# Windowed attention with a gated projection: each value product issued in three steps, one warm-up fewer, and a new written-out order

## The chip, the cores and the metric

The kernel runs on one core of one Trainium2 chip. The metric is the device time of one execution in microseconds (us). Five engines work side by side, each strictly in its own order: PE (matrix products; its weight loads are listed apart as PEld), DVE (vector), ACT (activations), POOL (here only a few fills at the start) and SP (issues the loads and most stores).

## What is computed

```
# attention: 8 batches, 8 heads, 512 local and 32 global positions, head size 64
s_g   = q_g @ [k_g, k_l].T / 8 ;      out_g = softmax(s_g) @ [v_g, v_l]
s_ll  = q_l @ k_l.T / 8, only where |i - j| <= 32
out_l = softmax([q_l @ k_g.T / 8, s_ll]) @ [v_g, v_l]
x     = [out_g, out_l] with the heads side by side        # 8 x 544 x 512
# gated projection
gate  = sigmoid(sum over k of conv_w[k] * x shifted by k)  # causal, 5 taps
out   = (gate * (x @ w_val)) @ w_out                       # 512 x 512 each
```

All of it is float32, but for `w_val`, `w_out` and `conv_w`, which arrive as float64 and are put into float32 parts by the kernel itself.

## The kernel before, in words

**Units of work.** The 64 pairs of batch and head are handled as 32 units `u` (two heads each, 128 partitions) and 16 windows `w` of two units. For a unit, PE makes the local scores (`s`, L385, and 8 mask products at L391 that stand at its end), DVE takes the maxima (`mx`, L396), ACT the exponentials (`exp`, L406), ACT or DVE scales them (`norm`, L421 or L423), and DVE transposes them in blocks of 32 (`t`, L429). For a window PE then makes the value product (`av`, L440): 160 small matrix instructions, each with a weight load of its own, one after the other over the ten slots of values. Copies take the result to SBUF (`xc`), it is split into a high and a low part (`xh`, `xl`, L489), and the five-tap convolution runs on DVE (`tap`, `conv`, L494). For units 0 and 1 alone PE makes the convolution (`pc`, L510) with diagonals that ACT writes (`dg`).

**Global queries.** Per batch: scores `gs` (L314), maximum `gmax` (L321, L322), exponentials `gexp` (L325), transposes on PE `gt` (L331) and their copies `gtc`, product with the values `gav` (L347), division `gden`, `grec`, `gnorm`, one more transpose `gx`.

**Weight products.** `g1.b.e.t` (L531) and `g2.b.r.e` (L555) are the two projections: three passes of 128x512 (high by high, low by high, high by low) per task, 280 tasks in all, most of the time of PE. Between them stand `gv`, `gh`, `gl` on DVE and ACT, and behind them the copies `ob` and the stores `st`. Before the first one can run, the two weight matrices are put together from their float64 words, eight tiles `w0` to `w7`, each by five steps on DVE (`s0` to `s4`, L206 to L214; `s0` may go to ACT, L204), a copy `high` and a difference `low` (L283).

**Order.** Nothing schedules itself. One long string of task names, `ORDER` (L60 to L148), is walked from front to back (L681), and each engine gets its instructions in that order. An `@` behind a name gives the PSUM banks of the task (of eight), and `:ACT` or `:DVE` the engine where a task may run on either. A load is issued on SP, and waits for the last PE instruction that stands ahead of it in the string (L245). `av` holds four half-used PSUM banks from its first instruction until both `xc` copies have read them. The names beginning with `z` are products of zeros (L624): they compute nothing, and are there to occupy PE. Two stand in the string of before, of six instructions each; two more stand ahead of it (L679).

```
        for name, *_ in LINE:
            if name[0] == "z":
                zeros(int(name.partition(".")[0][1:]), HOME[name][0])
            else:
                tasks[name]()
```

Of the kernel before, what the change touches and what calls it, by code (L numbers as in the profile page):

```python
# [61 lines left out]
gs0@06 w0.s1 rec1 w0.s2 gmax0 norm1.1:DVE ig2 iq4 exp0.0 exp3.0 exp0.1 w0.s3 iq5 norm1.0:ACT s2@2 den0 w1.s0:DVE gexp0.0
gt0.0@0 rec0 w0.s4 w0.high:ACT norm0.1:ACT t1 w0.low gtc0.0:ACT gexp0.1 ig3 exp3.1 norm0.0:DVE w1.s1 mx2 t0 gt0.1@0
w1.s2 w2.s0:DVE exp2.0 gtc0.1:ACT den3 w2.s1 rec3 w2.s2 w1.s3 w2.s3 norm3.1:DVE av0@46 exp2.1 den2 ig0 ig1 wi5 w2.s4
norm3.0:ACT xc0:ACT s5@0 w1.s4 xc1:ACT rec2 halo0 pc0.0@6 pc0.1 w2.high:ACT w1.high:ACT mx5 s4@2 w1.low iq7 norm2.1:ACT
w3.s0:ACT exp5.0 norm2.0:DVE t3 pc0.2 w2.low mx4 xh0:ACT w5.s0:DVE gav0@7 exp5.1 pc0.3 iq6 gden0 pc0.4 exp4.0 t2
conv0.3:ACT exp4.1 w3.s1 xl0 den5 grec0 av1@04 rec5 pc1.0@6 w3.s2 w5.s1 norm5.1:ACT w3.s3 xc3:ACT den4 w5.s2 wi6 w3.s4
ig6 wi4 rec4 gnorm0 xc2:ACT w3.high:DVE xh1:DVE s6@2 gs1@04 pc1.1 ig4 pc1.2 iv2 norm5.0:ACT norm4.0:ACT mx6 gmax1 xl1
gx0@7 exp6.0 gexp1.0 w3.low pc1.3 w5.s3 gexp1.1 gxc0:ACT tap2:ACT halo1:ACT pc1.4 exp6.1 ig5 tap3:DVE g1.0.2.0@7
g1.0.0.3@4 gt1.0@0 s7@2 iq9 conv2.0 iv3 w5.s4 w4.s0:ACT conv3.0 iq8 den6 conv1.3:ACT fix0 g1.0.1.2@5 t5 norm4.1:ACT  # L70
g1.0.3.3@6 rec6 gtc1.0:ACT mx7 norm6.0:ACT g1.0.2.2 g1.0.0.0 g1.0.1.0 exp7.0 conv2.1 w4.s1 conv3.1 w4.s2 t4 w5.high:ACT
w5.low g1.0.0.2 gt1.1@0 w4.s3 g1.0.1.3 g1.0.0.1 exp7.1 fix1 g1.0.1.1 gtc1.1:ACT conv3.2 w4.s4 g1.0.3.1 ig7 den7 av2@02
wi7 iq10 sig0 g1.0.2.3 g1.0.3.0 conv2.2 conv3.3 w4.high:ACT conv2.3 rec7 gv.0.1 norm6.1:ACT w6.s0:DVE xc4:ACT gv.0.0
sig1 s8@0 norm7.0:ACT xc5:ACT gh.0.0:ACT gav1@4 t6 ig11 w4.low iq11 mx8 g1.0.3.2 gl.0.0 g1.0.2.1 exp8.0 gden1 w7.s0:DVE
grec1 exp8.1 ig8 w7.s1 s9@2 gv.0.3 gnorm1 norm7.1:ACT mx9 ig9 gv.0.2 gs2@04 tap5:ACT gmax2 g2.0.3.0@6 t7 w6.s1 exp9.0
ig10 w7.s2 w6.s2 iv5 g2.0.0.0@7 den8 gexp2.1 gexp2.0 g2.0.3.1 g2.0.0.1 gx1@4 iq13 gxc1:ACT w7.s3 exp9.1 w6.s3 rec8
av3@04 gh.0.1:ACT den9 norm8.1:ACT w6.s4 tap4:DVE xc7:ACT halo2:ACT norm8.0:DVE rec9 g2.0.2.0@2 w7.s4 w6.high:ACT
g2.0.1.0@3 xc6:ACT g2.0.2.1 gl.0.1 iv4 conv4.0 gt2.0@4 t8 w6.low w7.high:ACT g2.0.1.1 gt2.1@0 iq12 gtc2.0:ACT w7.low
norm9.1:ACT xh2:ACT s10@4 g2.0.1.2 mx10 gtc2.1:ACT conv4.1 g2.0.2.2 g2.0.2.3 conv5.0 norm9.0:ACT halo3:ACT g2.0.3.2
exp10.0 xl2 g2.0.1.3 ob.0.1:ACT ob.0.2:ACT gav2@0 g2.0.0.2 exp10.1 g1.1.1.0@1 t9 conv5.1 conv4.2 g1.1.1.1 gden2 tap7:ACT  # L80
conv5.2 av4@24 den10 conv4.3 conv5.3 xh3:ACT grec2 rec10 sig2 g2.0.0.3 xc8:ACT tap6:DVE st.0.2:SP g2.0.3.3 xl3 st.0.1:SP
ob.0.0:ACT norm10.1:DVE gnorm2 s11@2 g1.1.0.2@0 conv6.0 xc9:ACT ob.0.3:ACT s13@4 g1.1.1.3 g1.1.0.3 mx11 s12@6
norm10.0:ACT st.0.3:SP iq14 st.0.0:SP t10 mx13 exp11.0 exp11.1 conv7.0 mx12 den11 exp13.0 g1.1.1.2 conv6.1 ig13 g1.1.0.0
gx2@2 iq15 g1.1.0.1 gxc2:DVE rec11 conv6.2 exp12.0 g1.1.2.1@3 exp13.1 norm11.1:DVE norm11.0:DVE conv6.3 t11 g1.1.2.0
exp12.1 g1.1.3.3@2 g1.1.3.1 conv7.1 den12 conv7.2 rec12 g1.1.2.2 conv7.3 g1.1.3.0 xh4:ACT sig3 av5@46 ig12 g1.1.2.3
xc11:ACT ig15 gv.1.1 g1.1.3.2 xc10:ACT gv.1.0 den13 norm12.1:ACT gh.1.0:DVE norm12.0:ACT gv.1.2 gs3@06 gl.1.0 iv6 iq16
s15@3 gv.1.3 g2.1.3.0@5 ig14 gmax3 g2.1.1.0@2 g2.1.3.1 gexp3.0 g2.1.1.1 gh.1.1:DVE gexp3.1 gt3.0@0 gt3.1@6 xh5:ACT rec13
gtc3.0:ACT norm13.0:ACT gtc3.1:ACT gl.1.1 g2.1.1.2 halo4:DVE tap8:ACT t12 g2.1.3.2 mx15 xl5 norm13.1:ACT s14@0 g2.1.3.3
conv8.0 g2.1.2.0@6 gav3@7 g2.1.2.1 ob.1.3:ACT tap9:ACT mx14 st.1.3:SP g2.1.0.0@5 t13 gden3 conv9.0 exp15.0 g2.1.1.3
grec3 conv9.1 iv7 iq17 exp14.0 g2.1.0.1 g2.1.2.2 exp15.1 gnorm3 g1.2.1.2@7 exp14.1 xl4 conv8.1 tap10:DVE conv9.2 conv8.2  # L90
g2.1.0.2 g1.2.1.1 gx3@3 gxc3:ACT ob.1.1:ACT den14 g1.2.1.3 halo5:ACT av6@03 conv9.3 tap11:ACT rec14 st.1.1:SP conv8.3
sig4 g2.1.2.3 ob.1.2:ACT g1.2.1.0 xc12:ACT xc13:ACT norm14.1:DVE g1.2.3.2@2 den15 conv11.0 s16@0 rec15 conv10.0
norm15.1:DVE norm15.0:ACT norm14.0:DVE gv.2.1 tap13:ACT mx16 s17@3 mx17 conv10.1 iq18 t15 g1.2.3.3 g1.2.0.0@7 g1.2.2.0@6
exp16.0 conv10.2 exp16.1 t14 conv11.1 exp17.0 ig18 g1.2.2.1 g1.2.3.1 st.1.2:SP iq19 g1.2.3.0 ig19 exp17.1 g1.2.2.3
g1.2.0.3 tap12:ACT conv10.3 g1.2.0.2 conv11.2 ig16 conv11.3 sig5 g2.1.0.3 av7@03 xc15:ACT xc14:ACT xh6:DVE g1.2.2.2
g1.2.0.1 den16 xl6 gv.2.3 gv.2.2 gv.2.0 xh7:ACT g1.3.1.0@4 gs4@02 xl7 gmax4 tap15:ACT halo6:ACT s18@6 ob.1.0:ACT
gh.2.0:ACT iv8 gexp4.1 mx18 iq21 iq20 rec16 st.1.0:SP gexp4.0 den17 ig17 g1.3.0.0@5 g1.3.1.1 gh.2.1:DVE gl.2.0 g1.3.1.2
g1.3.1.3 g1.3.0.1 halo7:ACT gt4.0@0 g1.3.0.3 norm16.1:ACT gtc4.0:ACT gl.2.1 conv13.0 conv12.0 tap14:DVE g2.2.3.0@2
exp18.0 conv12.1 exp18.1 s19@0 g2.2.0.0@3 g2.2.0.1 norm16.0:ACT rec17 mx19 norm17.1:ACT conv13.1 iq23 den18 t16 gt4.1@6
gtc4.1:ACT g2.2.0.2 g2.2.3.1 conv13.2 g2.2.3.2 conv12.2 norm17.0:ACT g2.2.3.3 exp19.0 ob.2.3:ACT t17 gav4@6 g2.2.0.3  # L100
conv13.3 conv15.0 conv12.3 exp19.1 conv15.1 ob.2.0:ACT conv14.0 gden4 g2.2.1.0@7 rec18 sig6 g2.2.1.1 conv14.1 grec4
den19 g1.3.0.2 g2.2.1.2 st.2.3:SP gnorm4 av8@02 ig20 norm18.1:ACT conv15.2 rec19 xc16:ACT iv9 xc17:ACT g1.3.3.1@6
g2.2.1.3 g1.3.3.3 conv14.2 gx4@2 norm19.0:DVE ig22 ob.2.1:ACT s21@0 st.2.1:SP norm19.1:ACT gv.3.1 conv15.3 s20@3 gv.3.0
g2.2.2.0@5 conv14.3 mx20 gxc4:ACT iv11 g1.3.3.2 norm18.0:ACT t19 sig7 exp20.0 g2.2.2.1 iq22 st.2.0:SP g2.2.2.2 g1.3.3.0
exp20.1 t18 gv.3.3 g1.3.2.0@2 mx21 g1.3.2.1 den20 halo8:ACT exp21.0 tap17:DVE g2.2.2.3 exp21.1 gh.3.0:DVE av9@63 gl.3.0
tap16:DVE g1.3.2.2 g1.3.2.3 xc19:ACT gs5@03 xc18:ACT rec20 conv16.0 norm20.1:DVE den21 gv.3.2 gmax5 iv10 xh8:ACT
gh.3.1:ACT s23@6 ob.2.2:ACT g2.3.3.0@2 g2.3.2.0@5 gl.3.1 st.2.2:SP g2.3.2.1 ig21 gexp5.1 iq26 mx23 rec21 gexp5.0 gt5.0@0
g2.3.2.2 ig23 halo9:ACT conv16.1 norm20.0:ACT t20 tap19:DVE norm21.0:DVE g2.3.3.1 xh9:ACT iq25 g2.3.2.3 g2.3.3.2 s22@3
exp23.0 gtc5.0:ACT conv17.0 ob.3.2:ACT mx22 norm21.1:ACT g2.3.3.3 xl9 g2.3.0.0@5 conv17.1 exp23.1 gt5.1@0 gtc5.1:ACT
iq24 g2.3.0.1 g2.3.0.2 ob.3.3:ACT t21 gav5@0 g2.3.0.3 exp22.0 st.3.2:SP conv17.2 st.3.3:SP xl8 conv16.2 iq27 den23  # L110
exp22.1 g1.4.0.2@1 den22 g2.3.1.0@2 g1.4.0.1 av10@36 g2.3.1.1 gden5 rec22 tap18:ACT grec5 rec23 ob.3.0:ACT conv18.0
g1.4.0.0 norm23.1:DVE gnorm5 conv17.3 norm23.0:ACT conv16.3 g2.3.1.2 conv19.0 norm22.1:DVE norm22.0:ACT xc20:ACT s24@3
st.3.0:SP ig27 ig25 conv18.1 xc21:ACT t22 s25@5 mx24 g1.4.0.3 sig8 mx25 g1.4.1.2@7 g1.4.1.1 gv.4.0 t23 exp24.0 conv19.1
conv19.2 g2.3.1.3 conv18.2 g1.4.1.3 conv18.3 exp24.1 ob.3.1:ACT exp25.0 den24 g1.4.1.0 conv19.3 av11@03 exp25.1
tap21:ACT iv13 g1.4.2.3@2 gv.4.1 gx5@5 xc23:ACT rec24 g1.4.2.2 g1.4.3.1@7 xc22:DVE gxc5:DVE tap22:DVE norm24.1:DVE
# [632 lines left out]
```

## Time and profile before

| What | us |
|---|---|
| median of 3 runs | 357.73 (355.07 to 360.5) |
| the profiled execution | 357.83 |
| its span, first to last instruction | 354.9 |
| outside the span | 2.9 |

The busy shares of the engines are taken over the span. PE runs its instructions in a pipeline, so that a PE that counts as busy need not be at its peak. "issue" as the end of a wait stands for time in which an engine waited for nothing that the profile shows.

### The profile page before, as it was taken

To read this page: it belongs to the slowest core of one execution; us is meant where nothing else is said; L and a number is where in the kernel's file an instruction comes from. 1 tells how busy PE (TensorE), PEld (TensorE's weight loads), DVE (VectorE), ACT (ScalarE), POOL (GpSimd) and SP (SyncE) were. 2 spreads that over 40 slices of the span, in tenths; PEclk is the share of its full clock that TensorE was granted. 3 is DMA by queue.
4 is the path that set the end of the run, shared out by engine and by line. 5 is a ranking of instruction groups with operands and counts; after the bars stand their busy time and mean duration, and the time that the engine had idled before them with its cause. 6 is when DMAs were issued, how large, how long until landed. Compare 5 with 4: busy or idle time off the path is not lost.

```text
span 354.9 us, 15327 instructions
## 1 busy us (share of the span) xinstructions
PE 328.3 (93%) x6736; PEld 255.5 (72%) x6736; DVE 304.5 (86%) x545; ACT 278.6 (78%) x887; POOL 1.0 (0%) x8
## 2 busy tenths in 40 slices
...
GB/s 278 376 234 43 178 102 267 243 220 265 159 64 125 195 180 175 100 216 125 225 128 258 149 268 136 86 144 209 170 116 21 175 154 86 2 30 31 60 89 90
DMA packets 19603, 54.75 MB, mean 154 GB/s; under 512 B 2128, under 2 KB 4560, under 8 KB 19536
## 3 DMA queue, kind: packets, MB, share of 16 engines
...
q8 instruction: 52, 0.85, 1.0%
...
## 4 chain that ended last, share of the span: by engine, by line
PE 72%; DVE 15%; ACT 5%; issue 4%; DMA 2%; SPq 0%; ACTq 0%; DVEq 0%
PE psum L555 23%; PE psum L531 22%; PE psum L440 10%; PE psum L385 7%; DVE gate L494 3%; PE psum L347 3%; DMA qk<-in_qk_dram 2%; DVE pts L429 2%; DVE mx L396 2%; PE psum L331 2%; PE psum L314 2%; PE psum L510 2%; DVE gm L321 1%; ACT pm L406 1%; DVE xl L489 1%
## 5 line engine op out<-in xcount | busy, mean ns | idle before, releaser
L406 ACT ACTIVATE pm<-psum,mx 128x128 f32<-128x128 f32 x256 | 90.7, 397 | 4.3 <-DVE mx L398 4.1
L494 DVE SCALAR_TENSOR_TENSOR gate<-xc,cw,gate 128x512 f32<-128x512 f32 x120 | 85.9, 741 | 1.4 <-ACT gate L230 1.1
L406 ACT ACTIVATION_READ_ACCUMULATOR pm<-psum,mx 128x1 f32 x256 | 60.5, 236 | 0.0
L555 PE MATMUL psum<-woh,gh 128*128 128x512 f32 x128 | 53.3, 416 | 0.0
L531 PE MATMUL psum<-xh,wvh 128*128 128x512 f32 x128 | 53.1, 415 | 0.0
L421 ACT ACTIVATE pm<-pm,mx 128x128 f32<-128x128 f32 x164 | 52.4, 413 | 0.4 <-DVE mx L415 0.4
L531 PE MATMUL psum<-xh,wvl 128*128 128x512 f32 x128 | 50.4, 394 | 0.0
L531 PE MATMUL psum<-xl,wvh 128*128 128x512 f32 x128 | 50.3, 393 | 0.0
L396 DVE TENSOR_REDUCE mx<-psum 128x8 f32<-128x1024 f32 x32 | 38.9, 1216 | 13.2 <-PE psum L391 13.2
L555 PE MATMUL psum<-woh,gl 128*128 128x512 f32 x128 | 50.2, 392 | 0.0
L555 PE MATMUL psum<-wol,gh 128*128 128x512 f32 x128 | 50.1, 392 | 0.0
L440 PEld LDWEIGHTS psum<-pts,v 32*64 32x64 f32 x2560 | 38.0, 135 | 15.1 <-issue 8.2
L440 PE MATMUL psum<-pts,v 32*64 32x96 f32 (+3 forms) x2560 | 42.8, 266 | 6.5 <-issue 5.4
L385 PE MATMUL psum<-qk 64*32 64x128 f32 x2048 | 38.1, 278 | 2.5 <-DMA qk<-in_qk_dram 1.3
L429 DVE STREAM_TRANSPOSE pts<-pm 128x1024 f32<-128x1024 f32 x32 | 39.6, 1238 | 0.2 <-ACT pm L421 0.2
L385 PEld LDWEIGHTS psum<-qk 64*32 64x32 f32 x2048 | 31.1, 107 | 11.8 <-issue 6.1
L555 PEld LDWEIGHTS psum<-woh,gh 128*128 128x128 f32 x128 | 24.1, 188 | 7.4 <-issue 2.2
L531 PEld LDWEIGHTS psum<-xh,wvh 128*128 128x128 f32 x128 | 24.0, 188 | 7.4 <-issue 1.6
L538 DVE TENSOR_TENSOR gv<-psum,gate 128x512 f32<-128x512 f32 x32 | 21.8, 685 | 7.8 <-PE psum L531 5.3
L236 ACT COPY ob<-psum 128x512 f32<-128x512 f32 x29 | 17.2, 601 | 14.2 <-PE psum L555 10.9
L531 PEld LDWEIGHTS psum<-xh,wvl 128*128 128x128 f32 x128 | 24.0, 188 | 5.7
L555 PEld LDWEIGHTS psum<-woh,gl 128*128 128x128 f32 x128 | 24.0, 188 | 5.4
(103 smaller groups left out, 485.1 us busy)
## 6 DMA issues: line engine op xcount, KB each, us to landing
...
```

Source lines behind the costliest of these rows:

```text
L236: A.copy(out, in_)
L347: on_pe(T.matmul(global_av(b)[SG * c:SG * c + SG, h, :], pgt[:, h, a, SG * c:SG * c + SG], vt[:, a, h, :], start=(a == 0), stop=(a == GS - ...
L385: on_pe(T.matmul(s[h][C * j:C * j + C, P * i:P * i + P], qkt[rows, C * m:C * m + C], keys, start=(i == 0), stop=False))
L396: V.tensor_reduce(out=mx[:, :8], in_=banks(f"s{u}", 2).rearrange("p h (i c) -> p (h i) c", i=R), axis=AX.X, op=ALU.max, negate=True)
L406: A.activation(out=pm[:, h, i, :], in_=st[u]["s"][h][:, P * i:P * i + P], func=AF.Exp, bias=mx[:, c:c + 1], scale=SCALE, accum_out=mx[:, 8 ...
L421: A.activation(out=p[:, i, :], in_=p[:, i, :], func=AF.Copy, scale=rec[:, i:i + 1])
L429: V.transpose(out=st[w, "pts"][:, :, R * k:R * k + R].rearrange("p h i a q -> p h (i a q)"), in_=st.pop(u)["pm"].rearrange("p h i c -> p h ...
L440: on_pe(T.matmul(x[j // 2][D * h:D * h + D, j % 2, C * first:C * (first + count)], vt[rows, slot, h, :], p, start=(slot == 0), stop=stop))
L494: V.scalar_tensor_tensor(out=acc, in0=st[w, "xc"][:, t, k:k + SL], scalar=cw[:, u % NDT, k:k + 1], in1=acc, op0=ALU.mult, op1=ALU.add)
L531: on_pe(T.matmul(bank(f"g1.{key}.{e}")[:, :n], w[:, e, t * P:t * P + P], x, start=(d == 1 and q == 0), stop=(d == NDT and q == 2)))
L538: V.tensor_tensor(out=box["gv", p][:, k], in0=bank(f"g1.{key}.{e}")[:, :n], in1=gates[w0 + p][:, k], op=ALU.mult)
L555: on_pe(T.matmul(o, g, w, start=(first and q == 0), stop=(last and q == 2)))
```

## The change

The value product of a window becomes three tasks, `ava`, `avb` and `avc`, over slots 0 to 2, 3 to 6 and 7 to 9. Their instructions are those of before, in the same order; but the string may put other PE work between the three.

```diff
+AV = (0, 1, 2), (3, 4, 5, 6), (7, 8, 9)
...
-    def l_av(w):
-        pts, vt = st.pop((w, "pts")), values.pop(w)
-        x = st[w, "x"] = [banks(f"av{w}", 2, t)[:, :, :SL // 2] for t in range(2)]
-
-        def product(j, h, slot, first, count, at, step, stop):
+    def l_av(w, part):
+        if part == 0:
+            st[w, "x"] = [banks(f"ava{w}", 2, t)[:, :, :SL // 2] for t in range(2)]
+        x, pts, vt = st[w, "x"], st[w, "pts"], values[w]
+
+        def product(j, h, slot, first, count, at, step):
...
-        for n in range(8):
-            j, h = n % R, (n + n // R) % 2
-            product(j, h, 0, 0, HB, R - 1, P, False)
-        for slot in range(1, NS):
+        for slot in AV[part]:
             for n in range(8):
                 j, h = n % R, (n + n // R) % 2
+                if slot == 0:
+                    product(j, h, 0, 0, HB, R - 1, P)
+                    continue
...
-        for name, fn in (("iv", load_v), ("av", l_av), ("halo", l_halo), ("xh", l_xh), ("xl", l_xl)):
+        for name, fn in (("iv", load_v), ("halo", l_halo), ("xh", l_xh), ("xl", l_xl)):
...
+        for n, part in enumerate("abc"):
+            tasks[f"av{part}{w}"] = lambda w=w, n=n: l_av(w, n)
```

The string itself is new throughout. Its first line of before and of after:

```diff
-iq0 iq1 iq2 iq3 wi0 iv0 wi1 iv1 wi2 wi3 cw z6.0@0 s1@0 mx1 dg0 s0@2 dg1 exp1.0 mx0 s3@4 mx3 z6.1@6 w0.s0:DVE exp1.1 den1
+iq0 iq1 wi0 iq2 iq3 wi1 iv0 iv1 wi2 wi3 cw z6.0@0 dg0 s1@0 mx1 s0@2 w0.s0:ACT ig3 ig0 w0.s1 w0.s2 exp1.0 w0.s3 exp1.1
```

Besides the order, some tasks change engine: of the `tap` 6 go from DVE to ACT, of the `ob` 4 from ACT to DVE, of the `w.high` 5 from ACT to DVE, of the `w.s0` 3 from DVE to ACT, of the stores 6 from SP to ACT's queue. The sigmoids stand in fewer groups: ACT changes between exponentials and sigmoids 13 times in the new string, 19 times in the old. The second group of zeros, `z6.1`, is gone.

Three places follow. On PE, near the start, before: the end of the third unit's scores (mask products), the zeros, and the first global scores (`gs0`).

```order
L391 LDWEIGHTS consts
L391 MATMUL psum<-consts 32x8x32
L626 MATMUL psum<-zr 128x512 x6
L314 MATMUL psum<-qk_93 32x272
L314 MATMUL psum<-qk_95 32x272
```

After, the first global scores stand right behind the second unit's mask products, and the third unit's scores behind them:

```order
L395 LDWEIGHTS consts
L395 MATMUL psum<-consts 32x8x32
L318 MATMUL psum<-qk_93 32x272
L318 MATMUL psum<-qk_95 32x272
L318 MATMUL psum<-qk_99 32x272
L318 MATMUL psum<-qk_101 32x272
```

Neither the third unit's scores nor the six products of zeros stand ahead of `gs0` any more.

On DVE, from the first maximum (`mx1`) to the first global maximum (`gm`); `wa` and `wraw` belong to the weight tiles. Before:

```order
L396 TENSOR_REDUCE mx_167<-psum 128x8
L398 TENSOR_SCALAR mx_167<-mx_167 128x8
L396 TENSOR_REDUCE mx_227<-psum 128x8
L398 TENSOR_SCALAR mx_227<-mx_227 128x8
L396 TENSOR_REDUCE mx_270<-psum 128x8
L398 TENSOR_SCALAR mx_270<-mx_270 128x8
L206 TENSOR_SCALAR wa_279<-wraw_101 128x512
L411 TENSOR_SCALAR mx_167<-mx_167 128x8
L209 TENSOR_SCALAR wa_279<-wa_279 128x512
L415 RECIPROCAL mx_167<-mx_167 128x8
L210 TENSOR_SCALAR wa_279<-wa_279 128x512
L321 TENSOR_REDUCE gm_305<-psum 128x1 x2
```

After:

```order
L400 TENSOR_REDUCE mx_173<-psum 128x8
L402 TENSOR_SCALAR mx_173<-mx_173 128x8
L213 TENSOR_SCALAR wa_216<-wa_216 128x512
L214 TENSOR_SCALAR wa_216<-wa_216 128x512
L216 SCALAR_TENSOR_TENSOR wa_216<-wraw_97,wa_216 128x512
L400 TENSOR_REDUCE mx_234<-psum 128x8
L402 TENSOR_SCALAR mx_234<-mx_234 128x8
L218 SCALAR_TENSOR_TENSOR wa_216<-wraw_97,wa_216 128x512
L242 CAST wvh<-wa_216 128x512
L287 TENSOR_TENSOR wvl<-wa_216,wvh 128x512
L325 TENSOR_REDUCE gm_271<-psum 128x1 x2
```

The third maximum has gone behind the first global one, and the whole of weight tile 0 now stands where it stood.

On PE, in the sixth value product (window 5; `pts` are the transposed exponentials). Before, its middle runs straight on:

```order
L440 MATMUL psum<-pts_1939,v_1387 64x96
L440 MATMUL psum<-pts_1939,v_1387 64x64
L440 MATMUL psum<-pts_1939,v_1387 64x96 x40
L440 MATMUL psum<-pts_1939,v_1387 64x64
L440 MATMUL psum<-pts_1939,v_1387 64x96
```

After, two weight products (three passes each) stand between its first and its second step:

```order
L445 MATMUL psum<-pts_1892,v_1371 64x96
L445 MATMUL psum<-pts_1892,v_1371 64x64
L536 MATMUL psum<-xh_1476,wvh 128x512
L536 MATMUL psum<-xl_1710,wvh 128x512
L536 MATMUL psum<-xh_1476,wvl 128x512
L536 MATMUL psum<-xh_1411,wvh 128x512
L536 MATMUL psum<-xl_1524,wvh 128x512
L536 MATMUL psum<-xh_1411,wvl 128x512
L445 MATMUL psum<-pts_1892,v_1371 64x96 x40
L445 MATMUL psum<-pts_1892,v_1371 64x64
```

Of the 16 value products 8 are parted by weight products in the new string, one by a transpose, and 7 run on as before.

## Rows read from the trace of the kernel before

**Rows 1.** The page: busy time, share of the span and instructions of each engine.

```profile
PE 328.3 (93%) x6736; PEld 255.5 (72%) x6736; DVE 304.5 (86%) x545; ACT 278.6 (78%) x887; POOL 1.0 (0%) x8
```

**Rows 2.** By stretch: length, then busy PE PEld DVE ACT POOL, PEclk, DMA share, GB/s.

```profile
9.90:57.80 47.90, 33.23 (x858) 21.37 (x858) 34.83 (x73) 37.07 (x152) 0.00 (x0) 0.82 0.57 192
57.80:350.70 292.90, 286.94 (x5722) 228.78 (x5721) 266.08 (x462) 236.97 (x725) 0.00 (x0) 1.00 0.44 144
```

**Rows 3.** PE in order of time, around the first weight product.

```profile
57.78 0.54 PE L531 MATMUL psum<-xh,wvh 128*128 128x512 f32 x1
```

**Rows 4.** The chain that ended last, 0 to 58 us: start, length, what.

```profile
11.40 3.28 issue
...
15.08 2.86 PE psum L626 x6
...
28.97 3.91 PE psum L440 x103
...
34.25 1.91 PE psum L510 x4
...
39.68 1.75 issue
...
45.57 3.28 issue
...
55.86 0.17 DVE gm L322
```

**Rows 5.** Waits of DVE from 9.9 to 57.8 us: total, times, longest.

```profile
DVE mx L396 <- PE psum L391: 6.1, 3, 3.9
DVE xh L238 <- ACT xc L236: 3.1, 1, 3.1
DVE gm L321 <- PE psum L314: 2.1, 1, 2.1
DVE gd L353 <- PE psum L347: 1.5, 1, 1.5
```

**Rows 6.** Groups of instructions: busy, mean ns of one, idle before.

```profile
L429 DVE STREAM_TRANSPOSE pts<-pm 128x1024 f32<-128x1024 f32 x32 | 39.6, 1238 | 0.2 <-ACT pm L421 0.2
L396 DVE TENSOR_REDUCE mx<-psum 128x8 f32<-128x1024 f32 x32 | 38.9, 1216 | 13.2 <-PE psum L391 13.2
L423 DVE TENSOR_TENSOR pm<-pm,mx 128x512 f32<-128x512 f32 x23 | 15.5, 685 | 0.0
L212 DVE SCALAR_TENSOR_TENSOR wa<-wraw,wa 128x512 int32<-128x512 int32 x8 | 5.3, 685 | 0.0
```

**Rows 7.** The chain later: score products, transposes, value products, three weight passes.

```profile
92.42 0.55 PE psum L331 x5
92.96 1.09 PE psum L385 x64
...
97.79 1.28 PE psum L347 x80
99.07 0.89 PE psum L555 x3
...
140.23 0.69 PE psum L531 x3
140.93 2.36 PE psum L440 x104
```

**Rows 8.** By stretch as in rows 2, up to the three stops of rows 4.

```profile
0.00:11.42 11.42, 9.35 (x223) 6.27 (x224) 4.92 (x13) 5.71 (x20) 1.05 (x8) 1.00 0.81 303
0.00:39.69 39.69, 28.30 (x732) 19.23 (x733) 26.63 (x57) 29.02 (x114) 1.05 (x8) 0.83 0.68 238
0.00:45.58 45.58, 32.44 (x860) 21.78 (x860) 31.02 (x69) 33.41 (x137) 1.05 (x8) 0.85 0.65 224
```

**Rows 9.** Waits of PE from 57.7 us on: total, times, longest.

```profile
PE psum L440 <- issue: 2.1, 2, 1.2
PE psum L314 <- ACT pm L406: 1.3, 2, 1.0
```

More of the change, by code (lines that the diff above doesn't have):

```diff
@@ L60 @@
 ORDER = """
-iq0 iq1 iq2 iq3 wi0 iv0 wi1 iv1 wi2 wi3 cw z6.0@0 s1@0 mx1 dg0 s0@2 dg1 exp1.0 mx0 s3@4 mx3 z6.1@6 w0.s0:DVE exp1.1 den1
[L62 to L115, printed above, removed]
@@ L146 @@
-g2.g.0.0@7 ob.7.1:DVE g2.g.1.0.0@6 gh.g.1:ACT g2.g.0.1 st.7.1:ACT gl.g.1 g2.g.1.0.2 ob.g.1.0:ACT g2.g.0.2 st.g.1.0
-g2.g.0.3 g2.g.1.1.0@6 g2.g.1.1.2 ob.g.0:ACT st.g.0 ob.g.1.1:ACT st.g.1.1
+iq0 iq1 wi0 iq2 iq3 wi1 iv0 iv1 wi2 wi3 cw z6.0@0 dg0 s1@0 mx1 s0@2 w0.s0:ACT ig3 ig0 w0.s1 w0.s2 exp1.0 w0.s3 exp1.1
+mx0 w0.s4 exp0.0 ig2 ig1 w0.high:DVE gs0@46 exp0.1 w0.low w1.s0:ACT gmax0 den0 den1 rec0 rec1 s2@0 gexp0.0 s3@2
+norm0.0:DVE norm0.1:ACT iq4 w1.s1 mx2 w1.s2 gexp0.1 norm1.1:ACT gt0.1@4 gt0.0@6 norm1.0:DVE w1.s3 t1 w2.s0:ACT
@@ new lines @@
+gtc0.0:ACT exp2.0 w2.s1 mx3 gtc0.1:ACT w1.s4 w2.s2 gav0@6 exp3.0 iq5 w1.high:DVE t0 exp2.1 w1.low gden0 w2.s3 ava0@40
+den2 grec0 exp3.1 w3.s0:ACT w2.s4 rec2 den3 norm2.1:DVE avb0 wi5 gnorm0 w2.high:DVE rec3 w3.s1 norm2.0:ACT norm3.0:ACT
+w2.low gx0@6 norm3.1:DVE ig4 avc0 xc0:ACT w3.s2 s4@2 t3 halo0 iq6 xc1:ACT pc0.0@7 xh0:ACT t2 gxc0:ACT dg1 pc0.1 ava1@04
+avb1 mx4 w5.s0:ACT iq7 exp4.0 xl0 exp4.1 avc1 pc1.0@6 w5.s1 w3.s3 w5.s2 w3.s4 xc2:ACT w5.s3 den4 pc1.1 w5.s4 w3.high:ACT
+xc3:ACT ig7 ig6 s5@0 tap2:ACT wi6 pc1.2 rec4 halo1:DVE w5.high:DVE w3.low xh1:ACT conv2.0 gs1@24 tap3:ACT norm4.0:ACT
@@ new lines @@
+wi4 mx5 conv2.1 conv3.0 exp5.0 gmax1 norm4.1:DVE exp5.1 pc1.3 pc1.4 den5 xl1 pc0.2 ig5 s6@0 iq9 gexp1.1 conv1.3:ACT rec5
+iv2 iv3 s7@4 mx6 gexp1.0 norm5.1:ACT gt1.0@2 pc0.3 pc0.4 g1.0.0.0@6 exp6.0 fix1 gtc1.0:ACT w4.s0:DVE t4 mx7 exp6.1
+norm5.0:DVE w5.low conv0.3:ACT fix0 gt1.1@2 den6 gtc1.1:ACT exp7.0 g1.0.0.3 t5 g1.0.3.3@0 g1.0.0.1 gav1@7 iq8 exp7.1
+conv2.2 w6.s0:DVE g1.0.1.3@1 conv3.1 gden1 iq11 sig0 w4.s1 g1.0.0.2 g1.0.1.0 conv2.3 grec1 g1.0.1.1 w4.s2 ava2@24 gnorm1
+rec6 den7 w4.s3 avb2 w6.s1 conv3.2 w4.s4 avc2 rec7 gx1@7 norm6.1:ACT g1.0.1.2 wi7 norm6.0:ACT gxc1:ACT norm7.1:ACT
```

110 lines of the change are left out of this document (78 added, 32 removed).

## The prediction

> **What bounds the kernel now.** The page comes first: PE is busy for 328.3 of 354.9 us, DVE for 304.5 [rows 1]. PE is so near to full that the time can only fall where PE stands still or runs slowly. The view by stretches says where that is. The first weight product starts at 57.78 us [rows 3]; from there to PE's last instruction at 350.7 us PE is busy for 286.94 of 292.90 us with its clock at the upper level throughout, so only 5.96 us are idle in it. Between 9.9 and 57.8 us PE is busy for 33.2 of 47.9 us at a mean granted clock of 0.82, and DVE for 34.8 [rows 2]. So the kernel is a start of some 58 us, in which the inputs of the first weight products are made, and a long body that PE fills. A start that is shorter by so much ends the body sooner by so much.
>
> What fills the start is read from the chain of waits and from DVE's waits. The chain holds three stops of PE with the end "issue" (3.28, 1.75 and 3.28 us), and the six products of zeros `z6.1`, 2.86 us, which run late, behind the first stop, so that `gs0` has to wait for them [rows 4]. DVE waits 12.8 us in all: 6.1 for local scores (3.9 of it once), 3.1 for ACT's copy before `xh1`, 2.1 for `gs0`, 1.5 for the first global value product [rows 5]. Each of these stands behind one of the stops or behind `z6.1`.
>
> **The change, part by part.**
>
> *The start.* I sum what DVE must do between the end of `mx1` (9.8 us) and the end of `gmax1`, the last maximum ahead of the first weight product in both orders. In the new order that is 62 tasks: 5 maxima (1.39 us with their scaling), 2 global maxima (1.6), 10 first steps of weight tiles (0.41), 10 later ones (0.68), 4 `high` (0.42) and 4 `low` (0.67), 4 `norm` (0.69), 4 transposes (1.24), one `xl` (1.2), 3 `conv` (0.74), and 15 small ones of about 0.18; 39.3 us with the means of the groups, of which the main kinds are shown [rows 6]. The same sum over the old order gives 37.7 us. The old stretch took until 56.0 us, when the scaling of `gmax1` ended [rows 4], less the 12.8 us of waits 33.4: neighbours overlap a little, and the sum has to be taken times 0.886. So the new stretch needs 34.8 us of DVE, and would end at 44.6 us without a wait, at 49.1 us with the overlap gone.
>
> Which waits are left? Behind `mx1` DVE now finds the whole of weight tile 0, whose first step ACT makes, so that the third scores are wanted only at about 17 us, and a stop of 3.28 us inside them is covered by `w0`, `gmax0` and two `norm`. `z6.1` is no longer ahead of `gs0`. `xh1` has gone to ACT, and with it the 3.1 us. The two loads of units 2 and 3 now stand behind a weight load of 512 KB; at the 303 GB/s of the first 11 us [rows 8] they land 1.7 us later than the 10 to 11 us at which the third scores ran, and `gs0`, which needs them, is wanted by DVE at 14 us: covered. I leave 2 us of waits in, so `gmax1` ends at 46.6 us. Behind it ACT makes `gexp1.1`, a copy and `gexp1.0` (2.1 us), PE `gt1.0` (0.55) and the two last convolution products (1.9) [rows 4, 7]: the first weight product at 51.2 us. PE has by then done `s7` and `gt1.0` too, which used to come later: 1.09 + 0.55 = 1.6 us. Gain 57.8 - 51.2 + 1.6 = 8.2 us.
>
> From this comes off what a stop costs. The trace shows where they fall: up to the first stop PE and PEld have run 223 + 224 = 447 instructions, up to the second 1465, up to the third 1720 [rows 8]. The distances are 1018 and 255, that is four times and once about 256 with a few semaphore instructions uncounted, so they come when a next block of 256 is not there. By the same count the new order has one such place (447 + 4 x 256) inside the middle step of its second value product, which lies close to DVE's path. I count half a stop, 1.6 us. The start gains 6.6 us. Bounds: 0, if half of DVE's waits return and a whole stop is on the path; 10, if neither is.
>
> The Trainium skill ("Runtime: NRT & Kernel Launch", section "Instruction fetch mechanics") has instructions fetched in blocks of 256, which agrees with the distances, and says that the fetch is hidden, since engines dispatch more slowly than blocks arrive; here three stops sum to 8.3 us, so the trace differs, and decides. By the page the 1.6 us would not come off, and the sum would end 1.6 us lower.
>
> *The value products in three steps.* No instruction is added, and a product of 2.36 us keeps its length in the sum. Two things change. First, more changes from small to large tiles: three weight passes take 0.69 us, but 0.89 right behind small ones [rows 7], 0.20 more. In the old order a weight product follows a small one 56 times, in the new one 61 times: +1.0 us. Second, the stops in the body: 2.1 us, two times, both inside a value product [rows 9]. Weight passes in between (0.23 us each, against 0.015 us for a small one) leave the next block more time; 8 of the 16 products are parted so. Of the 2.1 us I take 1 us off; bounds 0 and 2.
>
> *The body otherwise.* The rest of the idle 5.96 us are waits for ACT, the longest sum 1.3 us [rows 9]. In the new order DVE loses 10 us of waits at the start and PE gains 6.6, so DVE leads PE by some 3 us more, and ACT has six changes of function fewer. I take 2 us off; bounds -4, and +3 if the new order brings waits of its own. The tasks that change engine nearly cancel on DVE (6 `tap` of about 0.5 us go, 4 `ob` and 2 `gh` of 0.7 come), and DVE is no bound.
>
> *The sum*, against the profiled execution: 357.83 - 6.6 + 1.0 - 1.0 - 2.0 = 349.2 us. That execution stands 0.1 us from the median of the runs (357.73), so nothing is added. I round to 349.5.
>
> **The rivals.**
>
> *The lead is lost.* The start is a string of dependencies over four engines, and I followed DVE alone. If a stop falls on the second value product in full (3.28 us) and the loads of units 4 and 5, issued only behind the global value product, hold `s4` for another 2 us, the gain of the start is 6.6 + 1.6 - 5.3 = 2.9 us; with the body as it was, 357.8 - 2.9 + 1.0 = 355.9 us. For it: two of the three old stops stood behind global or value products. Against: DVE has work before each.
>
> *All of it comes.* No stop on the path, 8.2 + 1 us at the start, and 5 us of the body's idle time: 357.8 - 9.2 + 1.0 - 5 = 344.6 us. For it: the waits of the body name ACT, which has less to do in the new order. Against: the place of the counted stop lies inside dense small work.
>
> *Slower: PE's clock in the start.* In the old order the first value product took 3.91 us at the lower level (1.2 GHz), against 2.36 at the upper [rows 4, 7], after PE had stood nearly still. The new order takes six products away there. From `gs0` to the first weight product PE has, at the upper level, 8 score blocks at 1.09, 10 convolution products at 0.96, 3 transposes at 0.55, two value products at 2.36 and one global one at 1.28: 25.9 us [rows 4, 7], for which 40 us are there (11.5 to 51.2). So the clock decides once its mean there is under 0.65. At 1.2 GHz throughout it is 51.8 us: the first weight product at 63.3 us, 5.5 us later than now, less the 1.6 us done ahead: 357.8 + 3.9 + 1.0 = 362.7 us. Against it: the mean was 0.82 in the old start, idle time and all [rows 2]. The Trainium skill ("TensorE: Matmul & The Clock Gate", Part 1) has an idle PE fall to half its clock and work bring it back; the two lengths of the value product agree, and it speaks against taking a warm-up away.
>
> **How the numbers follow.** The forecast, 349.5 us, has 0.48, with a range of its own of 346.5 to 352.5. The lost lead has 0.28, the full gain 0.16, the slow clock 0.08. A measurement of this kernel tells about 2% from no change, that is 350.6 and 364.9 us. Below 350.6 lie some 0.7 of the forecast and the full gain: 0.34 + 0.16 = 0.50. Above 364.9 lies half of the slow clock, 0.04. The rest, 0.46, is within 2%. The range that leaves out no more than 2 in 10 goes from the full gain to just beyond the lost lead: 344 to 357.
>
> **What would show it.** Right: the first weight product at 50 to 54 us; DVE's waits before it under 4 us; no stop behind the third unit's scores that DVE waits for; PE's idle time behind the first weight product about 3 us; value products parted by weight products, with three passes behind small ones still at 0.89 us. Wrong: a first weight product after 56 us (lost lead), a mean granted clock under 0.65 in the start (slow clock), or a body whose idle time is above 6 us, which would say that the new order has waits of its own.

## The result, and the profile after

The changed kernel takes 340.25 us (median of 4 runs, 340.02 to 340.9). The kernel before took 359.07 us beside it (4 runs, 355.07 to 360.5). The ratio is 0.955, with a 95% interval of 0.9485 to 0.9615: faster by 4.5%, and by about twice what was forecast. It is taken against the two faster of the four runs of before (355.07 and 357.73 us), since the other two, over 1.5% above the fastest, count as slow; against these two the gain is 16 us. The profiled execution of the changed kernel took 340.45 us, with a span of 338.7 us; that of before took 357.83 us.

PE's row of the page, which answers to [rows 1]:

```profile
PE 325.7 (96%) x6730; PEld 253.9 (75%) x6730; DVE 306.1 (90%) x545; ACT 272.5 (80%) x878; POOL 1.0 (0%) x8
```

PE has six instructions fewer (the second `z6`), nearly the same busy time, and 16 us less of span around it. Next the view by stretches, cut at the first weight product as in [rows 2] (length; busy PE, PEld, DVE, ACT, POOL; PEclk; DMA share; GB/s), with one piece of the start by itself:

```profile
9.90:49.50 39.60, 32.98 (x929) 21.61 (x929) 38.62 (x83) 38.77 (x154) 0.00 (x0) 0.87 0.77 257
49.50:334.80 285.30, 284.74 (x5646) 227.26 (x5644) 263.61 (x452) 229.43 (x717) 0.00 (x0) 1.00 0.44 145
...
20.00:30.00 10.00, 7.92 (x244) 6.24 (x244) 9.50 (x22) 9.22 (x43) 0.00 (x0) 0.56 0.52 188
```

The start is 8.3 us shorter, and DVE and ACT both fill it now (38.6 and 38.8 of 39.6 us). In the body PE's idle time fell from 5.96 us to 285.30 - 284.74 = 0.56 us. The first weight product, which answers to [rows 3]:

```profile
49.49 0.80 PE L536 MATMUL psum<-xh,wvh 128*128 128x512 f32 x1
```

DVE's waits between 9.9 and 49.5 us, against 12.8 us in [rows 5], and PE's waits from there on, against [rows 9] (total, times, longest):

```profile
DVE mx L415 <- ACT pm L410: 0.4, 1, 0.4
```

```profile
PE psum L445 <- issue: 0.5, 1, 0.5
```

One wait of DVE and one of PE are all that these views list. Last a piece of the chain that ended last, with one value product in two pieces; it answers to [rows 7]:

```profile
166.03 1.86 PE psum L445 x80
167.88 0.90 PE psum L536 x3
...
171.67 0.76 PE psum L445 x35
172.43 1.09 PE psum L389 x64
...
173.62 0.89 PE psum L536 x3
```

A parted value product costs PE 1.86 + 0.76 = 2.62 us, against 2.36 whole, and three passes behind small products still cost 0.90 us, against the 0.69 of [rows 7].

Where the 17.4 us between the two profiled executions went, beside the terms of the forecast:

| part | forecast | measured |
|---|---|---|
| first weight product earlier | 5.0 (57.8 to 51.2, less half a stop) | 8.3 |
| PE's busy time in the body | 0.6 (1.6 done ahead, 1.0 of switches) | 2.2 |
| PE's idle time in the body | 3.0 (1.0 in value products, 2.0 other) | 5.4 |
| behind PE's end, and outside the span | 0 | 1.5 |
| sum | 8.6 | 17.4 |

No term went the other way, and none explains the gap alone. The table tells where time went between two orders that differ in everything; it doesn't tell which part of the change did it. That is what the experiments are for.

### The profile page after: what moved, and what is told of

Read it like the earlier page. It is cut to its first block, busy times and chain, and to the rows that moved or that the text cites. A ratio compares the mean times of both kernels' runs of the same rounds, so it can differ in the third digit from the quotient of the medians.

```text
span 338.7 us, 15326 instructions
## 1 busy us (share of the span) xinstructions
PE 325.7 (96%) x6730; PEld 253.9 (75%) x6730; DVE 306.1 (90%) x545; ACT 272.5 (80%) x878; POOL 1.0 (0%) x8
## 3 DMA queue, kind: packets, MB, share of 16 engines
q1 hardware_dynamic: 17664, 50.90, 45.6%
## 4 chain that ended last, share of the span: by engine, by line
PE 92%; DMA 5%; SPq 1%; issue 0%; ACT 0%
PE psum L536 29%; PE psum L560 29%; PE psum L445 12%; PE psum L389 9%; PE psum L351 3%; PE psum L515 3%; DMA vg<-in_vgw_dram 3%; PE psum L318 3%; DMA qk<-in_qk_dram 2%; PE psum L335 2%; SPq L251 1%; PE psum L395 1%; PE psum L369 0%; ACT obg L240 0%
## 5 line engine op out<-in xcount | busy, mean ns | idle before, releaser
L410 ACT ACTIVATION_READ_ACCUMULATOR pm<-psum,mx 128x1 f32 x256 | 57.8, 226 | 0.0
L536 PE MATMUL psum<-xh,wvh 128*128 128x512 f32 x128 | 53.8, 420 | 0.0
L425 ACT ACTIVATE pm<-pm,mx 128x128 f32<-128x128 f32 x160 | 50.6, 413 | 1.3 <-DVE mx L415 0.6
L445 PE MATMUL psum<-pts,v 32*64 32x96 f32 (+3 forms) x2560 | 44.0, 264 | 0.5 <-issue 0.5
L400 DVE TENSOR_REDUCE mx<-psum 128x8 f32<-128x1024 f32 x32 | 38.8, 1213 | 5.1 <-PE psum L395 5.0
L389 PE MATMUL psum<-qk 64*32 64x128 f32 x2048 | 39.0, 273 | 2.6 <-issue 1.0
L389 PEld LDWEIGHTS psum<-qk 64*32 64x32 f32 x2048 | 30.7, 105 | 12.8 <-issue 5.3
L240 ACT COPY ob<-psum 128x512 f32<-128x512 f32 x27 | 15.8, 598 | 22.6 <-PE psum L560 21.6
L536 PEld LDWEIGHTS psum<-xl,wvh 128*128 128x128 f32 x128 | 24.1, 188 | 4.5 <-issue 0.2
```

The lines of the kernel that those rows point to most:

```text
L240: A.copy(out, in_)
L389: on_pe(T.matmul(s[h][C * j:C * j + C, P * i:P * i + P], qkt[rows, C * m:C * m + C], keys, start=(i == 0), stop=False))
L400: V.tensor_reduce(out=mx[:, :8], in_=banks(f"s{u}", 2).rearrange("p h (i c) -> p (h i) c", i=R), axis=AX.X, op=ALU.max, negate=True)
L410: A.activation(out=pm[:, h, i, :], in_=st[u]["s"][h][:, P * i:P * i + P], func=AF.Exp, bias=mx[:, c:c + 1], scale=SCALE, accum_out=mx[:, 8 ...
L425: A.activation(out=p[:, i, :], in_=p[:, i, :], func=AF.Copy, scale=rec[:, i:i + 1])
L445: on_pe(T.matmul(x[j // 2][D * h:D * h + D, j % 2, C * first:C * (first + count)], vt[rows, slot, h, :], p, start=(slot == 0), stop=(slot ...
```

## The experiments

Ratios are to the kernel before, run on the same chip; intervals are of 95%. Times are medians, but every profile shows one execution. What is written in the order can be moved without touching the rest, so most of the kernels differ from the one before or after in that string alone.

### Is the parting of the value products worth anything?

**The changed order, value products whole.** Steps two and three follow the first at once:

```diff
-... ava2@24 gnorm1 rec6 den7 w4.s3 avb2 w6.s1 conv3.2 w4.s4 avc2 rec7 ...
+... ava2@24 avb2 avc2 gnorm1 rec6 den7 w4.s3 w6.s1 conv3.2 w4.s4 rec7 ...
```

> The changed kernel with the three steps of every value product put back together at the place of the first step; nothing else differs. Lead theory (the shorter start lets VectorE and ScalarE run ahead, and that alone empties the body of waits): PE's idle time behind the first weight product stays under 1.5 us, some 0.2 us per saved change from small to large tiles comes back, time 338.5 to 341.5 us. Split theory (the weight products between the steps give the next block of instructions time to arrive): stops of 1 to 3 us appear inside value products, idle time 3 us or more, time 343 to 346 us.

Measured: 351.2 us (4 runs, 349.3 to 352.75), ratio 0.9872 (0.9805 to 0.9938): slower than either theory had it. Of the gain of 4.5%, 1.3% is left; 11 us are gone. The first weight product starts at 49.15 us, so the start is untouched. PE's waits behind it, and PE in order of time around two of the value products (start, length, what, count; in brackets the idle time ahead):

```profile
PE psum L446 <- issue: 8.4, 8, 2.0
PE psum L537 <- issue: 0.6, 1, 0.6
PE psum L446 <- ACT gate L523: 0.5, 1, 0.5
```

```profile
168.59 2.10 PE L446 MATMUL psum<-pts,v 32*64 32x256 f32 x131
172.03 0.53 PE L446 MATMUL psum<-pts,v 32*64 32x96 f32 x29 [1.34 <-issue]
...
178.93 2.12 PE L446 MATMUL psum<-pts,v 32*64 32x256 f32 x135 [0.51 <-ACT gate L523]
182.47 0.51 PE L446 MATMUL psum<-pts,v 32*64 32x96 f32 x25 [1.42 <-issue]
```

The products stand still in their middle, with all their operands there ("issue"): after 131 of 160, and again after 135. Hardly anything else makes PE wait. So the new order has DVE and ACT ahead of PE through nearly the whole body, and without the parting it pays some 9 us for stops. What such a stop is, the traces show below, in "The stop by itself".

**The same pair behind the old start.** First the order of before up to its first weight product, then the changed one with parted products; then the same with whole ones.

```diff
-(the changed order, all of it)
+(the order of before up to the first g1, then all tasks not yet named, as the changed order has them)
```

> The order of the kernel before up to the first weight product, and from there the order of the changed kernel. Lead theory: first weight product at 57 to 59 us, and 3 to 6 us of idle time behind it, since VectorE and ScalarE have no lead; time 353 to 357 us. Body theory: first weight product as late, idle time behind it under 1.5 us, time 349.5 to 352 us.

Parted: 354.36 us (10 runs), ratio 0.9936 (0.9893 to 0.9978), as the lead theory had it.

> The old start with the new order behind it, as in the kernel that took 354.4 us, but with every value product whole at the place of its first step. With the new start the same joining cost 11 us (340.25 to 351.2). Theory that the stops depend on what PE executes around a value product and not on when the first weight product ran: idle before value products put down to issue rises from nearly nothing to 6 to 9 us in the profile, 361 to 366 us. Rival that stops and other waits stand for each other, so that behind the old start, whose late operands make PE wait anyway, joining costs little: idle in the body no more than 3 us above the 2.8 us of the parted one, 354 to 358.

Whole: 363.7 us (4 runs, 363.09 to 367.17), ratio 1.024 (1.0143 to 1.0338), slower than the kernel before, and as the theory had it that ties the stops to what PE executes around a value product. The rival, that behind the old start other waits take the place of the stops, missed. PE's waits in the body, whole and then parted:

```profile
PE psum L446 <- issue: 8.3, 6, 2.3
PE psum L446 <- ACT pm L411: 1.6, 2, 0.9
PE psum L446 <- DVE pts L434: 0.9, 1, 0.9
```

```profile
PE psum L445 <- ACT pm L410: 1.6, 2, 0.9
PE psum L445 <- DVE pts L433: 0.9, 1, 0.9
```

The stops come and go with the parting (8.3 us and none); the other waits, at the seam of the two orders, stay to a tenth. Behind either start the parting is worth about the same: 363.7 - 354.4 = 9.3 us and 351.2 - 340.25 = 11.0 us. And in the new order the new start is worth 12.5 us with whole products (363.7 to 351.2) and 14.1 with parted ones, though a part of this is the seam's 2.5 us of waits.

### What is the start worth by itself?

**The kernel before without its second warm-up.**

```diff
-... mx3 z6.1@6 w0.s0:DVE ...
+... mx3 w0.s0:DVE ...
```

> The kernel before without its second group of zeros, z6.1; nothing else differs. Lead theory: the zeros held up the first global scores by 2.9 us on the path, but the three stops stay, so 2 to 3 us faster than before: 355 to 357.5 us against 359.1. Warm-up theory (the zeros were the main loss of the start): 5 us or more faster, 354 or less. If the zeros were of use to PE's clock: mean granted clock between 10 and 58 us below 0.78, and no gain or a loss.

Measured: 355.95 us (10 runs), ratio 1.0025 (0.9989 to 1.0062): no change. In its profile the first weight product starts 6 us earlier, at 51.64 us, but the body takes 296.35 us in place of 292.90, and PE's stops inside value products are 4.5 us in place of 2.1. What is left in the profile doesn't show between the medians: this execution took 354.71 us, the shortest of its ten runs.

**The new start, then the order of before with whole products.**

```diff
-(the order of before, all of it)
+(the changed order up to the first g1, less s7 and gt1.0, then all tasks not yet named but z6.1, as the order of before has them)
```

> The changed kernel's order up to the first weight product (less the eighth local scores and one global transpose), and from there the order of the kernel before, value products unparted. Lead theory: first weight product at 48 to 51 us as in the changed kernel, idle time of PE behind it under 2 us, time 341 to 344 us. Body theory (the new order of the body removes its waits, whatever the start): first weight product as early, but 4 to 6 us of idle time behind it, time 346 to 350 us.

Measured: 354.58 us (10 runs), ratio 0.9963 (0.9925 to 1.0002), slower than either theory had it. The first weight product starts at 48.71 us, 9 us earlier than before, and the body takes 298.22 us in place of 292.90. PE's waits of the first in it:

```profile
PE psum L446 <- issue: 4.0, 4, 2.2
PE psum L336 <- ACT pm L411: 1.7, 2, 0.9
PE psum L390 <- issue: 1.3, 2, 1.1
PE psum L319 <- DMA qk<-in_qk_dram: 0.9, 1, 0.9
```

PE's stops, 2.1 us in [rows 9], have grown to 5.3 (4.0 and 1.3), and with other waits PE idles 9.4 us in place of 6.0. In the profile the longer body takes back 5.3 of the 9 us; between the medians 1 us is left of them, since this execution is the shortest of its ten (352.97 us) and the profiled one of before stands above the median of the 25 runs beside it (357.83 against 355.53). That the old order was laid out for a later PE is how I read it; no run changed that alone.

### Does parting help in any order?

**The order of before, 13 of 16 products parted** by up to three weight products that stood ahead of them, so that the first step begins earlier; and **the same behind the new start**.

```diff
-... g1.0.0.1 g1.0.1.1 ... g1.0.3.1 ... av2@02 ...
+... ava2@02 g1.0.0.1 g1.0.1.1 avb2 g1.0.3.1 avc2 ...
```

> The order of the kernel before, with 13 of its 16 value products parted: up to three weight products that stood just ahead of a value product are moved between its steps; nothing else differs, the zeros stay. Block theory (PE stops when a next 256 instructions are not there in time, which takes some 3.3 us from the start of a block; a whole value product is run through faster): stops inside value products behind the first weight product fall from 2 or more us to under 0.7, the start keeps its stops, 2 to 5 us faster than before. Rival (the parting is worth little without the shorter start, since waits for ScalarE and VectorE take the place of the stops): under 1.5 us faster.

> The run e3_newstart (new order up to the first weight product, old order behind it) with the same 13 value products parted. Block theory: what the new start gained was given back as stops in whole value products; parted, the stops go, idle time behind the first weight product falls from 10 to under 4 us, time 344 to 349 us, some 6 to 9 us below e3_newstart. Rival (the rest of the new order is what counts): within 2 us of e3_newstart.

Measured: 382.17 us (4 runs), ratio 1.0755 (1.0674 to 1.0836), and 377.07 us (4 runs), ratio 1.0605 (1.0531 to 1.068). Both expectations missed by far in time. PE's waits of the first in its body:

```profile
PE psum L445 <- ACT pm L410: 4.0, 5, 1.8
PE psum L318 <- DMA qk<-in_qk_dram: 2.1, 1, 2.1
PE psum L445 <- issue: 1.7, 4, 0.6
PE psum L445 <- ACT pgt L240: 1.6, 1, 1.6
PE psum L445 <- DVE gd L361: 1.1, 1, 1.1
```

A first step that stands earlier waits for ACT and DVE. The stops did shrink, and by more than the line of 1.7 us says: only 0.6 us of it follows an instruction packet as the stops below do, and 1.1 us stands at the start of a first step, long behind any packet. The page counts 55.3 us of busy time for its value products, against 44.0 in the changed kernel: six of the 48 products of a first step take 1.34 us in one place (at 159.35 us), while ACT's exponentials are on the chain that ended last. That they wait there for these, too briefly to be listed, is how I read it.

**Parted by what stands behind them**, on the kernel with the new start and the old order, so that no product begins earlier. In the order nine of fourteen are parted; the expectation says eight.

```diff
-... ava2@02 avb2 avc2 g1.0.2.3 g1.0.3.0 ...
+... ava2@02 g1.0.2.3 g1.0.3.0 avb2 avc2 ...
```

> The new start with the old order behind it (354.6 us with whole value products), and eight of fourteen value products parted by one to three weight products that stood behind them, so that no product begins earlier than it did; the steps behind the first begin up to 1.5 us later. Theory that a stop needs a run of small products and that the earlier parting lost by starting value products before their operands were there: the stops inside value products fall from 4.0 us in the profile to 1.5 to 2.5, no new waits for ACT before value products, 352 to 354.5. Rival that parting costs by itself whatever is moved (more switches, longer products): 360 or more. Rival that nothing changes: 354 to 355.5, with 4 us of stops still inside value products.

Measured: 361.25 us (4 runs, 360.37 to 362.84), ratio 1.0152 (1.0087 to 1.0217). A miss again: 6.7 us slower than with whole products. Some of PE's waits in its body, to be held against the kernel with the new start above:

```profile
PE psum L319 <- DMA qk<-in_qk_dram: 2.3, 1, 2.3
PE psum L446 <- issue: 2.0, 2, 1.1
...
PE psum L352 <- issue: 1.4, 1, 1.4
PE psum L390 <- issue: 1.3, 3, 0.7
```

The stops inside value products halved, from 4.0 to 2.0 us, as the theory of stops has it, but another came (1.4 us in a global value product), so that the sum of stops hardly fell: 4.7 us against 5.3. The body is 9.1 us longer; 2.1 of this is idle time, and 7 us are busy time, 3.3 of it in the value products (45.6 us against 42.3, though one product's mean length is the same), which I can't assign. What stands: in each order tried parting took stops out of the value products, and it paid only in the changed one.

### The stop by itself

**Twelve whole value products and nothing else**, then **the same with 24 loads of 592 KB** issued behind the first product. Both leave out scores, softmax, gate and projections; the output is one copy of the last product.

```diff
-        for name, *_ in LINE:
-            ...
+        for n in range(12):
+            l_av(0, 0)
+            l_av(0, 1)
+            l_av(0, 2)
+            ...
+                for u in range(0):   # 24 in the second
+                    ... nc.sync.dma_start(t, qk[u]) ...
```

> All but one thing left out: one tile of values is loaded, the transposed exponentials are zeros, and PE makes 12 whole value products (3840 instructions) one behind the other, with no load in flight; one block of the output is stored. Block theory: a stop at about every 256th instruction, 1.2 to 1.6 us each, so that a block takes 3.2 to 3.6 us and the 12 products 42 to 50 us instead of 28.3. Rival (the stops come only from the loads that the instruction blocks share the queues with): no stops, 28 to 30 us.

> As e8_dense, with 24 loads of 592 KB started behind the first product, so that the queues are full while PE works. Block theory: the stops are as many as in e8_dense and longer, 1.5 to 4 us each. Rival (loads alone make the stops): stops here and none in e8_dense. If loads play no part: the same as e8_dense within 0.3 us a stop.

One run each: 63.4 and 78.48 us. The first, PE in order of time and its waits:

```profile
13.87 1.73 PE L445 MATMUL psum<-pts,v 32*64 32x32 f32 x128 [1.42 <-issue]
17.32 2.06 PE L445 MATMUL psum<-pts,v 32*64 32x64 f32 x128 [1.73 <-issue]
20.78 2.08 PE L445 MATMUL psum<-pts,v 32*64 32x96 f32 x128 [1.39 <-issue]
24.50 2.08 PE L445 MATMUL psum<-pts,v 32*64 32x96 f32 x128 [1.64 <-issue]
28.23 2.03 PE L445 MATMUL psum<-pts,v 32*64 32x96 f32 x128 [1.64 <-issue]
...
PE psum L445 <- issue: 21.0, 14, 1.7
```

It stops after each 128 products, which with a weight load each are 256 instructions, whatever the place in the value product. From one stop to the next it takes 3.45 or 3.73 us (13.87 to 17.32, 24.50 to 28.23), of which the products need 1.7 to 2.1. The twelve products take 52.7 us, somewhat above the 42 to 50 that were expected.

What PE waits for at "issue" is in the trace too. Queue q8, of the kind "instruction", is apart from that of the loads (q1), and each of its packets has 16 KB; the page of this run lists 14 of them, as many as there are stops. This is the view of the DMA queues from 14 to 22 us, where a slice is 0.2 us:

```profile
GB/s 0 0 0 0 82 0 0 0 0 0 0 0 0 0 0 0 0 0 0 0 0 0 82 0 0 0 0 0 0 0 0 0 0 0 0 0 0 0 0 82
q8 instruction: 3, 0.05, 2.6%
```

Its packets start at 15.00, 18.44 and 21.95 us, some 1.1 us behind the start of a block, and take 1.0 to 1.3 us; PE goes on 1.2 to 1.6 us after a packet has landed, here and at each of the 13 stops of the run with loads. The same holds in the whole kernels: at the five stops of the kernel before (three in its start, two in value products) PE goes on 1.3 to 1.5 us after such a packet, at those of over 0.5 us in the changed order with whole products 1.3 to 1.6 us (the packet of the stop that ended at 182.47 us landed at 181.14), and in none of the fourteen traces do two packets of q8 start less than 3.29 us apart. So these stops are waits for a block of instructions. With the loads in flight:

```profile
16.77 2.73 PE L445 MATMUL psum<-pts,v 32*64 32x32 f32 x128 [4.44 <-issue]
22.69 3.39 PE L445 MATMUL psum<-pts,v 32*64 32x64 f32 x128 [3.19 <-issue]
27.52 3.21 PE L445 MATMUL psum<-pts,v 32*64 32x96 f32 x128 [1.44 <-issue]
...
65.02 1.73 PE L445 MATMUL psum<-pts,v 32*64 32x32 f32 x128 [1.42 <-issue]
```

```profile
12.30:16.77 4.47, 0.03 (x2) 0.00 (x1) 0.00 (x0) 0.00 (x0) 0.00 (x0) 1.00 1.00 390
50.40:53.80 3.40, 3.36 (x128) 3.07 (x128) 0.00 (x0) 0.00 (x0) 0.00 (x0) 0.50 0.02 5
```

At some 390 GB/s the stops are 1.4 to 4.4 us, and once the loads have ended and the clock is up they are 1.4 to 1.7 again. The longest came at a granted clock of 1.00 (first line), so the lower clock isn't what made it. The packets themselves took no longer (0.92 to 1.24 us); they started later, 20.22 us for the block that PE had begun at 16.77. So a stop needs no load, and in this one run it was longer beside loads. The products themselves are slower where the granted clock was at its lower level: 3.36 us for a block at 0.50 when the loads had ended (second line), against 2.06. The Trainium skill ("Runtime: NRT & Kernel Launch", section "Instruction fetch mechanics") has blocks of 256 instructions, with which the distance agrees. The Trainium skill calls the cost of crossing from one to the next "mostly hidden"; for products as short as these the trace differs, with 1.4 to 1.7 us a block.

### The warm-ups

**The changed kernel with the second warm-up back**, and **without the first one too**.

```diff
-... w0.high:DVE gs0@46 ...
+... w0.high:DVE z6.1@6 gs0@46 ...
```

```diff
-... cw z6.0@0 dg0 ...
+... cw dg0 ...
```

> The changed kernel with the second group of six zero products put back where it stood, ahead of the first gating scores. What is asked is whether the warm-up that the change left out cost or gave anything in the new order. Theory that PE waits there anyway: in the profile of the changed kernel PE has idle stretches between 9.9 and 25 us (0.8, 0.7, 1.8, 0.9 and 1.2 us) and DVE is what bounds the start, so 6 products of about 0.5 us, some 3 us, fit beside it and the time stays within 1 us of 340.25: 339.5 to 341.5, first weight product at 49.5 to 50. Rival that PE's three microseconds come on top, since six of its twelve instructions stand ahead of gating scores that DVE waits for: 342.5 to 344, first weight product at 51.5 to 53. Rival that it keeps the granted clock up between 20 and 30 us, where the changed kernel shows 0.56: 338 to 339.5.

> The changed kernel without the first group of six zero products too, so without any warm-up. Theory that the start is bound by DVE and ACT and that PE's clock there does not matter: 340 to 341, first weight product at 49.2 to 49.9, the granted clock lower in the first 10 us. Rival that the first scores, which DVE waits for at 6 to 9 us, run at the lower clock: about 1 us of scores twice as long, 341 to 342.5. Rival that twelve instructions less move the block borders and bring a stop back in the body: 341.5 to 344, with an idle stretch of over 1 us before value products or scores in PE's waits.

Measured: 340.11 us (4 runs, 339.71 to 340.59), ratio 0.9554 (0.95 to 0.9608), and 343.5 us (4 runs, 342.14 to 344.3), ratio 0.9646 (0.9574 to 0.9719). The second warm-up is worth nothing in the new order. Leaving out the first costs some 3.3 us (343.5 against 340.25); the two intervals overlap a little, the runs don't. Without it PE's second scores, at 8 us, run at the lower clock (0.50 from 8.1 to 10 us); here they are, in the kernel without it and in the changed one, and with the former a stop in its second value product:

```profile
8.10 1.89 PE L389 MATMUL psum<-qk 64*32 64x128 f32 x56
...
37.80 1.21 PE L445 MATMUL psum<-pts,v 32*64 32x96 f32 x79 [1.26 <-issue]
```

```profile
7.91 1.05 PE L389 MATMUL psum<-qk 64*32 64x128 f32 x59
```

The first weight product then starts at 51.52 us, 2.0 us later. The lower clock and the stop come together here, so how much of the loss is due to each isn't shown. No kernel tried beats the changed one by what can be measured.

## Why the prediction was wrong

**The step that failed** is the price of the parting: "Of the 2.1 us I take 1 us off; bounds 0 and 2." I read the stops off the body of before, and took them as all there were. The new order, with the same products whole, has 8.3 to 9 us of them, and the parting is worth 9.3 and 11.0 us, some five times my upper bound. With whole products the new order takes 351.2 us, 1.7 from the forecast and inside my range; it is the parting that takes the measurement out of it. The forecast changed the order and did not ask which stops the new one would have without the parting.

Why the new order has more stops than the old one is only in part shown. One reading is that stops and other waits stand for each other: a PE that waits for an operand gives the next block the time to arrive. The old body fits it: its stops were 2.1 us, and 4.8 and 5.3 where PE reached it 6 and 9 us earlier. The new body does not: whole products have 8.3 us of stops behind the old start, which kept 2.5 us of other waits, and 9.0 behind the new one. So the order itself counts for more, and what in it brings the stops stays open.

**The start.** The mechanism held in the main: DVE is full in it, though ACT is too, and no run tells which of the two bounds it. The first weight product came at 49.49 us, against 51.2 us without a stop and 52.8 with half of one. Two cautions fell away. DVE waited 0.4 us, where I had left in 2. And no stop fell into the second value product, in which I had counted one:

```profile
34.27 2.62 PE L445 MATMUL psum<-pts,v 32*64 32x256 f32 x160
```

That value product runs whole in the changed kernel, and without a stop. The count was right all the same. The second stop of before came after 1465 instructions [rows 8]. In the kernel without the first warm-up the stop in this product came after 732 and 732, that is 1464 (first line below). The changed kernel passes the same count inside the same product, between the second line and the third:

```profile
0.00:37.79 37.79, 24.86 (x732) 17.34 (x732) 31.05 (x68) 31.01 (x121) 1.04 (x8) 0.86 0.75 266
0.00:34.25 34.25, 25.73 (x657) 17.38 (x657) 27.53 (x61) 27.51 (x105) 1.05 (x8) 0.85 0.79 283
0.00:36.90 36.90, 28.39 (x818) 19.83 (x818) 30.14 (x66) 30.16 (x118) 1.05 (x8) 0.86 0.76 273
```

There the packet had landed at 34.17 us, before the product began; in the other kernel it landed at 36.55, and PE went on at 37.80. The count tells where a stop can come, and the time at which the block arrives whether it does.

**"A start that is shorter by so much ends the body sooner by so much"** is the sentence on which the sum stood. The kernel without its second warm-up and the one with the new start alone refute it for the old order: 6 and 9 us earlier, 0 and 1 us at the end. In the changed order with parted products the start does reach the end: the profile with the old start took 350.9 us, and of the 10.5 us to 340.45 the first weight product has 6.4 (55.85 to 49.49) and the waits at the seam 2.5.

**The switches.** 0.90 us behind small products, as forecast at 0.89. **The other waits** of the body: I took 2 of 3.9 us off, and all of them went.

**Not foreseen at all:** 1.5 us behind PE's last instruction and outside the span. No run was aimed at it; the time outside the span is 1.8 us in most of these kernels, those with the old order among them, so I don't put it down to the change.

**The rivals.** The lost lead didn't come. That all of it would come, 344.6 us, was the nearest, for a reason that I did not have. The slow clock came for 10 us only: 0.56 from 20 to 30 us, but 0.87 over the start, where that rival wanted a mean under 0.65. DVE was busy for 9.50 of those 10 us; in the kernel with the warm-up back the clock there was 0.66, and the time the same (340.11 us). That rival also doubled all of PE's work at the lower level; a block of value products took 3.36 us there against 2.06, 1.6 times as long.

**What stays open:** what in the new order makes whole products stop so often; the 7 us of busy time in the kernel parted by what stands behind; and why the kernels with the old order differ by some 5 us from run to run (353.85 to 358.49 for the kernel before in the last comparison), the changed one by 0.9. That stops of varying length make that spread would fit the dense products, but no run showed it.
